# A Fourier mixing and ELU kernel on one core: where the first weight pieces are summed, where two buffers are cleared, and the order of scratch writes and x loads

## The chip, the cores and the metric

The kernel runs on one core of one Trainium2 chip. A core has a matrix engine (TensorE, PE in the profile; its weight loads are PEld), VectorE (DVE), ScalarE (ACT), GpSimd (POOL) and SyncE (SP), which here only issues transfers; 16 DMA engines move the data. The metric is the device time of one execution in microseconds (us).

## What is computed

The reference is a Fourier filter along the sequence followed by a two-layer block with an ELU between the layers:

```python
X = np.fft.rfft(x, axis=1)                     # x: 8 x 3008 x 256
y = np.fft.irfft(X * (filt_r + 1j * filt_i), n=3008, axis=1)
h = y.reshape(24064, 256) @ w_in               # 256 x 2048
g = np.where(h > 0, h, np.exp(np.minimum(h, 0)) - 1)
out = g @ w_out                                # 2048 x 256
```

w_in and w_out arrive as float64. The kernel turns them into float32 itself, from the two 32-bit halves of each number.

## The kernel before

**Batches and quads.** The 8 batches go through two halves: the filter, and the two-layer block. The second half is the long one and runs without pause; the filter of batch b + 1 is spread over it. The block is cut into items (b, m, q): 8 batches, 6 groups of tokens m, 4 quarters q of the 2048 hidden columns. The program calls the place of an item in that list a *quad*; 24 quads make a batch (`PER`), and a quad takes about 13 us. In quad i TensorE runs the seven up products of item i (`up_steps`: Strassen-like, L541) interleaved with the seven down products of item i - 1 (`down_steps`, L623). The letters U and D in L981 and L990 give the interleaving. Each quad's VectorE work contains four adds that rebuild blocks of h from products (L549: b11, b22, b21 and so on), four ELU maxima (L563), and four operations that prepare the next factors (L599 to L603); ScalarE copies products out of PSUM (L552) and computes the exponentials (L558, L559). The add of b22 (L549) reads the product accumulated in `phd`, and TensorE's last up product of the quad (s4) goes on accumulating into the same bank: TensorE waits for that add.

**A plan written by hand.** Everything else is put into quads with `at(quad, place, function, ...)`. Place 2 comes after the third of the U and D steps of the quad, place 3 after the fifth, place 0 in the middle, place 1 at the end. Within the program all engines follow program order, each its own instructions, so the plan decides what stands ahead of what on VectorE, ScalarE, POOL and SP.

**Weights.** They come in 16 pieces k = 4q + j. For j of 0 and 1 a piece belongs to `w_in[q]`, for 2 and 3 to `w_out[q]`. `w_fetch(k)` loads it; `w_split(k)` (L708, L709, VectorE) separates mantissa and exponent bits; `w_float(k, *parts)` (L718, ScalarE) has four steps numbered 0 to 3 that turn them into floats; `w_join(k, parts)` (L724 to L739, VectorE) puts sign and exponent together (part 0) and multiplies into the weight tile (part 1); `w_sums(k, engine, parts)` (L743 to L750) makes the four sums that the Strassen-like scheme needs, on 128 x 256 each, on the engine given. In the first 85 us (the *boot* part) batch 0 goes through the filter on its own while pieces 0 to 11 are made; pieces 12 to 15 are finished in quads 0 to 3. Piece 11's sums are used by the down products in quad 3, piece 13's by the up products in quad 3, piece 15's by the down products in quad 4.

**The filter of later batches.** For batch b, with t = 24 (b - 1): `x_load(b, c)` (L199 to L215) loads one of six slices c with seven transfers on SP (one table, six, or five, of x); `x_unit` (L217) makes a sum and a difference on VectorE; `a_unit` (L227) multiplies two slices on TensorE (psa) and ScalarE copies the result out (L238); `z_write` (L302) writes it to a scratch tensor z in DRAM with two transfers on SP. The slices lie in four buffers, so a load has to wait until `a_unit` has read the slice that is four earlier. When all six slices are written, `z_read` (L310) reads z transposed, eight transfers for two groups, and `b_unit` (L375) multiplies them on TensorE with 40 small matmuls (pf, L383) in quad t + 6. `f_read` (L321) reads the filter on POOL into the buffers `fbufs`, two of which have to be zero outside the rows that are read; `f_pairs` (L771) prepares that filter in DRAM with transfers on SP in quads 1 to 4. For batch 1 the units of slices 0 to 5 lie in quads 2, 2, 3, 3, 4, 4; for later batches in t + 0, 0, 3, 3, 4, 4.

The loop that the change reorders stands at L937 to L945: per slice it plans x_unit, a_unit for every second slice, then the load of the slice four ahead, then the scratch write.

**The end of the boot part.** `y_write_first(g)` (L365) writes the filter's result to the scratch yd; its last transfer is issued by ScalarE. `y_read(0, 0)` (L473) and `n_unit(0, 0)` (L483, matmuls psn, evictions y at L492) follow, then `n_sums` (L516 to L519, VectorE), and with quad 0 the two-layer block begins. Seven warm-up matmuls (L901) stand between.

Of the kernel before, what the change touches and what calls it, by code (L numbers as in the profile page):

```python
# [28 lines left out]
B = 8  # L29
# [4 lines left out]
NXC = H // XC  # L34
NG = K2 // 4
XBUFS = 4
# [95 lines left out]
def kernel(  # L132
# [9 lines left out]
    nc = tc.nc  # L142
# [34 lines left out]
    fbufs = [fall[:, i] for i in range(FBUFS)]  # L177
# [502 lines left out]
    def w_fetch(k, queue=nc.gpsimd):  # L680
        q, j = divmod(k, 4)

        if k in (3, 4, 14, 15):
            wd = t2[:, k % 11 - 3].rearrange("p u d -> p (u d)")
        elif k == 10:
            wd = t1p.tile([P, XC, D], FP32, tag="t1", name="wd").rearrange("p u d -> p (u d)")
        elif k in (6, 7, 8, 9):
            wd = xp.tile([P, 2, 2, D], FP32, tag="xc", name="wd").rearrange("p k u d -> p (k u d)")
        else:
            wd = fbufs[{5: 0, 11: 0, 12: 1, 13: 2}.get(k, k)].rearrange("p c u d -> p (c u d)")  # L690
        wd = wds[k] = wd.bitcast(U32).rearrange("p (a w) -> p a w", w=2)
        if j < 2:
            srcs = [moe_w_in.bitcast(U32)[ts(j, P), ts(q, 1024)]]
        else:
            srcs = [moe_w_out.bitcast(U32)[ts(4 * q + 2 * (j - 2) + i, P), :] for i in range(2)]
        for i, s in enumerate(srcs):
            n = 512 // len(srcs)
            queue.dma_start(wd[:, ts(i, n), :].rearrange("p a w -> p (a w)"), s)
# [6 lines left out]
    def w_split(k):  # L705
        m, e, f, l = wts[k] = wtmp[{9: 2, 10: 1, 11: 0, 12: 3, 13: 4, 15: 5}.get(k, k % 2)]
        hi = wds[k][:, :, 1]
        nc.vector.tensor_scalar(out=m, in0=hi, scalar1=0x000FFFFF, scalar2=None, op0=ALU.bitwise_and)  # L708
        nc.vector.tensor_scalar(out=e, in0=hi, scalar1=0x7FF00000, scalar2=None, op0=ALU.bitwise_and)  # L709

    def w_float(k, *parts):
        m, e, f, l = wts[k]
        ef = e.bitcast(FP32)
        steps = ((l, wds[k][:, :, 0], AXT.Identity, 2.0 ** -52, 0.0), (f, m, AXT.Identity, 2.0 ** -20, 1.0),
                 (ef, e, AXT.Relu, -8.0, edges[:, 0:1]), (e, ef, AXT.Relu, -1.0, edges[:, 1:2]))
        for i in parts or range(4):
            o, x, func, scale, bias = steps[i]
            nc.scalar.activation(out=o, in_=x, func=func, scale=scale, bias=bias)  # L718

    def w_join(k, parts=(0, 1)):  # L720
        q, j = divmod(k, 4)
        m, e, f, l = wts[k]
        if 0 in parts:
            nc.vector.scalar_tensor_tensor(out=e, in0=wds.pop(k)[:, :, 1], scalar=0x80000000, in1=e,  # L724
                                           op0=ALU.bitwise_and, op1=ALU.bitwise_or)
            nc.vector.tensor_tensor(out=f, in0=f, in1=l, op=ALU.add)
        if 1 not in parts:
            return
        e = e.bitcast(FP32)
        if j < 2:  # L730
            f, e = (t.rearrange("p (a j c) -> p a j c", a=2, j=2) for t in (f, e))
            dst = w_in[q][:, 2 * j:2 * j + 2, :, :].rearrange("p j a c -> p a j c")
            nc.vector.tensor_tensor(out=dst, in0=f, in1=e, op=ALU.mult)
        else:

            f, e = (t.rearrange("p (i a e s) -> p i e a s", i=2, a=4, e=2) for t in (f, e))
            dst = w_out[q][:, 0:4, j - 2, :].rearrange("p (i e) (a s) -> p i e a s", i=2, a=4)
            for i in range(2):
                nc.vector.tensor_tensor(out=dst[:, i], in0=f[:, i], in1=e[:, i], op=ALU.mult)  # L739
        if j % 2 == 1 and k < 7:  # L740
            w_sums(k)

    def w_sums(k, engine=nc.vector, parts=(0, 1, 2, 3)):  # L743
        q, j = divmod(k, 4)
        w = (w_in if j < 2 else w_out)[q]
        a11, a21, a12, a22, s1, s2, s4 = (w[:, i] for i in range(7))
        sums = ((s1, a21, a22, ALU.add), (s2, s1, a11, ALU.subtract), (s4, a12, s2, ALU.subtract), (a21, a11, a21, ALU.subtract))
        for i in parts:
            o, x, y, op = sums[i]
            engine.tensor_tensor(out=o, in0=x, in1=y, op=op)  # L750
# [30 lines left out]
    with tc.manual_schedule():  # L781


        with tc.tile_pool(name="boot", bufs=1) as bp:
# [68 lines left out]
            c = t1p.tile([P, XC, D], FP32, tag="t1", name="wfl").rearrange("p (a b) d -> p a (b d)", a=2)  # L853
            places(c[:, 0], flat(tnp.tile([P, 4, P], FP32, tag="tn", name="we")), c)
            for t in (zq, rq):
                t = t.rearrange("p a u d -> p a (u d)")
                places(t[:, 0], t[:, 1], t[:, 2:4])
            t = t3f.rearrange("p a (b u) d -> p (a b) (u d)", u=2)
# [1 line left out]
            w_split(7)  # L860
            w_join(6)
            w_split(8)
            floats = {0: (7, 0, 1), 1: (7, 2, 3), 2: (8, 0, 1), 3: (8, 2, 3), 4: (9, 0, 1), 5: (9, 2, 3), 6: (10, 0, 1), 7: (10, 2, 3)}
            for g in range(4):
                t_first(g)
            for g in range(NG + 2):
# [20 lines left out]
            y_read(0, 0, slice(0, K2 - 4), slice(K2 - 4, K2))  # L887
            for k in (14, 15):
                w_fetch(k, nc.sync)
            w_join(8)  # L890
            for k in (11, 12, 13):
                w_split(k)
# [2 lines left out]
            w_sums(9)  # L895
            w_join(10)
            w_join(11)
            w_sums(11, nc.gpsimd)
            warm = psO.tile([P, 512], FP32, tag="po2", name="warm")
            for k in range(7):  # L900
                nc.tensor.matmul(warm, w_in[0][:, 0, 0, :], w_in[0][:, 0:2].rearrange("p a b c -> p (a b c)"),  # L901
# [15 lines left out]
        def at(quad, place, fn, *a):  # L917
            plan.setdefault((quad, place), []).append((fn, a))


        for quad, place, fn, *a in ((0, 0, w_split, 14), (1, 2, w_join, 12), (1, 2, w_split, 15), (1, 2, w_float, 14, 0, 1),
                                    (1, 3, w_float, 14, 2, 3), (2, 2, w_float, 15, 0, 1), (2, 3, w_float, 15, 2, 3),
                                    (2, 0, w_join, 14, (0,)), (2, 1, w_join, 14, (1,)), (2, 1, w_join, 15),
                                    (3, 0, w_sums, 15, nc.vector, (0, 1, 2)), (3, 1, w_sums, 15, nc.vector, (3,))):
            at(quad, place, fn, *a)
        for c in range(2, XBUFS):
# [3 lines left out]
            for u in range(2):  # L930
                at(1 + 2 * c + u, 0, f_pairs, c, u)
        for i in range(2):
            at(2 + i, 1, nc.gpsimd.memset, fbufs[i], 0.0)
        for b in range(B):
            t = (b - 1) * PER
            if b > 0:
                for c, s in enumerate((2, 2, 3, 3, 4, 4) if b == 1 else (0, 0, 3, 3, 4, 4)):  # L937
                    at(t + s, 0, x_unit, b, c)
                    if c % 2 == 0:
                        opens.add(t + s + 1)  # L940
                        at(t + s, 1, a_unit, b, c)
                    nb, nxt = (b, c + XBUFS) if c + XBUFS < NXC else (b + 1, c + XBUFS - NXC)
                    if nb < B:
                        at(t + s, 1, x_load, nb, nxt)
                    at(t + s, 1, z_write, b, c)  # L945
                for g in range(0, NG, 2):
                    s = t + 6 + 2 * g
                    opens.update((s + 1, s + 4))
                    for k in (g, g + 1):
                        at(s - 2, 1, f_read, b, k)  # L950
                        at(s - 1, 0, z_read, b, k)
                    at(s, 1, b_unit, b, g)
                    at(s + 1, 2, re_mult, b, g)
                    at(s + 1, 1, re_sums, b, g)
                    parts = ((0, 0), (0, 1), (1, 0), (1, 1))
                    early = 3 if g == 6 else 4
                    at(s + 2, 2, im_mult, b, g, *parts[:early])
                    at(s + 2, 1, im_mult, b, g, *parts[early:])
                    at(s + 2, 1, im_join, b, g)
                    at(s + 3, 2, im_sums, b, g)  # L960
                    at(s + 3, 1, bi_unit, b, g)
                    at(s + 3, 1, y_write, b, g)
            for m, (s, place) in enumerate(((23, 0), (25, 1), (29, 1), (32, 0), (36, 0), (40, 0))):
                if b > 0 or m > 0:
                    at(t + s - 2, 0, tn_read, b, m)
                    at(t + s - 2, 1 if m == 0 else 0, y_read, b, m)
                    at(t + s, place, n_unit, b, m)

                    at(*((t + s + 1, 1) if m > 2 else (t + s, place)), n_sums, b, m)
                if b == 0 and m == 1:  # L970
                    at(1, 1, w_join, 13)
                    at(1, 1, w_sums, 13, nc.gpsimd)
                at(t + PER + 4 * m + 5, 0, c_unit, b, m)
                at(t + PER + 4 * m + 6, 0, o_unit, b, m)

        items = [(b, m, q) for b in range(B) for m in range(6) for q in range(4)]
        for i in range(-PER, len(items) + 3):
# [3 lines left out]
            for n, k in enumerate("DUUDUDDU" if i in opens else "UUDUDDU"):  # L981
                s = ups if k == "U" else downs
# [7 lines left out]
            for k in "DUUDUD" if i in opens else "DUUDUDD":  # L990
                s = ups if k == "U" else downs
# [40 lines left out]
```

## Time and profile before

| what | value |
|---|---|
| median of the runs | 2592.95 us (runs: 2590.71, 2592.95, and a disturbed one of 9503.64) |
| the profiled execution's own time | 2593.74 us |
| its span, first to last instruction | 2591.9 us |
| mean granted TensorE clock | 0.993 of full |
| TensorE busy | 2551.7 us, 98% |
| VectorE, ScalarE, POOL busy | 79%, 60%, 7% |
| DMA, mean | 80 GB/s |

How to read the profile lines below. A line of the timeline has the start in us from the span's start, the duration in us, the engine (SPq and ACTq are the queues that issue transfers), the source line, the operation, output<-input by the program's names, shape, and the number of instructions that were merged; in brackets stands how long the engine had been idle and what it waited for. Matmuls are pipelined and their ends are modelled. A line of the windows has the window, its length, then busy time and number of instructions of PE, PEld, DVE, ACT and POOL, the granted clock, the busy share of the DMA engines and the GB/s.

### The profile page before, as it was taken

How to read it: one execution, taken by the hardware profiler on the slowest of the kernel's cores; microseconds unless marked ns; L12 is line 12 of the kernel's file. 1: busy time of each engine (PE TensorE's matmuls, PEld its weight loads, DVE VectorE, ACT ScalarE, POOL GpSimd, SP SyncE). 2: the span in 40 equal slices, each digit the busy share in tenths (PEclk: the TensorE clock that was granted, in tenths of full speed). 3: DMA queues.
4: the chain of work that ended last, by engine and by line, in shares of the span. 5: the costliest groups of instructions: out<-in, count | busy, mean ns of one | idle time of the engine just before them, and what ended most of it. 6: DMA issues, size and time to landing. Idle time of an engine off the chain costs nothing.

```text
span 2591.9 us, 39471 instructions
## 1 busy us (share of the span) xinstructions
PE 2551.7 (98%) x14474; PEld 2204.0 (85%) x14474; DVE 2041.2 (79%) x3524; ACT 1548.1 (60%) x2713; POOL 169.1 (7%) x325
## 2 busy tenths in 40 slices
PE   6899999999999999999999999999999999999998
PEld 4688889888898888988889888888889888898887
DVE  6868887788877888788886888778887788866666
ACT  6755556656566655665556656566655655555554
POOL 5100100010000000000000000000000010000000
PEclk8999999999999999999999999999999999999999
DMA  9662213422234231433215231243213322110010
GB/s 282 169 184 69 70 36 88 129 70 63 51 100 108 61 78 42 119 81 76 62 44 151 63 84 37 78 122 84 61 43 87 91 60 68 37 49 20 21 29 17
DMA packets 229177, 206.35 MB, mean 80 GB/s; under 512 B 128666, under 2 KB 195418, under 8 KB 228984
## 3 DMA queue, kind: packets, MB, share of 16 engines
q1 hardware_dynamic: 213624, 172.94, 26.2%
q0 software_dynamic: 14000, 30.44, 4.3%
q8 instruction: 114, 1.87, 0.3%
q10 hardware_dynamic: 1360, 0.46, 0.1%
q14 instruction: 79, 0.65, 0.1%
HBM read 131.87 MB, written 78.17 MB: 81 GB/s over the span
## 4 chain that ended last, share of the span: by engine, by line
PE 96%; DMA 2%; DVE 1%; ACT 0%; issue 0%; SPq 0%; DVEq 0%; ACTq 0%
PE po L623 44%; PE phs L541 25%; PE phd L541 13%; PE pha L541 6%; PE psn L490 3%; PE psa L234 2%; PE pf L383 2%; PE pv L455 1%; DMA xc<-in_x_dram 1%; DMA x<-in_x_dram 0%; PE po L330 0%; DMA yd<-t 0%; PE po L296 0%; PE psr L330 0%; DMA t<-yd 0%
## 5 line engine op out<-in xcount | busy, mean ns | idle before, releaser
L623 PE MATMUL po<-g,wo 128*128 128x256 f32 (+1 forms) x5376 | 1315.1, 377 | 0.0
L623 PEld LDWEIGHTS po<-g,wo 128*128 128x128 f32 x5376 | 1013.6, 190 | 163.6 <-issue 49.7
L552 ACT ACTIVATE g<-phs 128x512 f32<-128x512 f32 (+1 forms) x576 | 339.0, 589 | 751.6 <-PE phs L541 750.2
L559 ACT ACTIVATE e<-e 128x512 f32<-128x512 f32 (+1 forms) x768 | 477.2, 621 | 24.4
L549 DVE TENSOR_TENSOR g<-phd,g 128x512 f32<-128x512 f32 (+1 forms) x384 | 259.6, 676 | 293.6 <-ACT e L559 205.1
L541 PE MATMUL phs<-ys,wi 128*128 128x256 f32 (+1 forms) x1536 | 387.6, 375 | 2.0 <-ACT g L552 1.5
L541 PE MATMUL phs<-y,wi 128*128 128x256 f32 (+1 forms) x1536 | 388.5, 375 | 0.0
L563 DVE SCALAR_TENSOR_TENSOR g<-e,g 128x512 f32<-128x512 f32 (+1 forms) x576 | 387.3, 672 | 0.3 <-ACT e L559 0.2
L558 ACT ACTIVATE e<-g 128x512 f32<-128x512 f32 (+1 forms) x576 | 353.4, 614 | 46.7 <-DVE g L549 38.1
L541 PEld LDWEIGHTS phs<-ys,wi 128*128 128x128 f32 x1536 | 291.4, 190 | 36.0 <-ACT g L552 3.0
L541 PEld LDWEIGHTS phs<-y,wi 128*128 128x128 f32 x1536 | 288.2, 190 | 35.8 <-ACT g L552 0.2
L563 DVE SCALAR_TENSOR_TENSOR g<-e,phs 128x512 f32<-128x512 f32 (+1 forms) x192 | 130.0, 677 | 140.3 <-ACT e L559 139.9
L541 PE MATMUL phd<-ys,wi 128*128 128x256 f32 (+1 forms) x768 | 196.2, 378 | 3.1 <-DVE g L549 3.1
L541 PE MATMUL pha<-y,wi 128*128 128x256 f32 (+1 forms) x768 | 194.0, 375 | 0.0
L541 PE MATMUL phd<-y,wi 128*128 128x256 f32 (+1 forms) x768 | 193.7, 375 | 0.0
L558 ACT ACTIVATE e<-phs 128x512 f32<-128x512 f32 (+1 forms) x192 | 113.0, 589 | 128.7 <-PE phs L541 128.7
L541 PEld LDWEIGHTS phd<-ys,wi 128*128 128x128 f32 x768 | 145.0, 191 | 24.1 <-DVE g L549 8.2
L541 PEld LDWEIGHTS pha<-y,wi 128*128 128x128 f32 x768 | 145.6, 190 | 17.5 <-ACT y L492 0.2
L541 PEld LDWEIGHTS phd<-y,wi 128*128 128x128 f32 x768 | 145.8, 190 | 16.5
L324 POOL DMA_DIRECT2D fall<-fp x224 | 110.5, 501 | 733.4 <-DVE r L428 704.3
L549 DVE TENSOR_TENSOR g<-pha,g 128x512 f32<-128x512 f32 (+1 forms) x192 | 129.3, 673 | 25.9 <-PE pha L541 25.7
L600 DVE TENSOR_TENSOR g<-g,g 128x512 f32<-128x512 f32 (+1 forms) x192 | 130.7, 681 | 6.6
(155 smaller groups left out, 2097.8 us busy)
## 6 DMA issues: line engine op xcount, KB each, us to landing
yd<-t SPq DMA_DIRECT2D x127, 192.0 KB
t<-yd SPq DMA_DIRECT2D x47, 512.0 KB
z<-t SPq DMA_DIRECT2D x84, 256.0 KB
fall<-fp POOLq DMA_DIRECT2D x224, 96.0 KB, 3.0
t<-z SPq DMA_DIRECT2D x224, 96.0 KB
out_dram<-o SPq DMA_DIRECT2D x632, 32.0 KB
tn<-tn_t SPq DMA_DIRECT2D x48, 256.0 KB
xc<-in_x_dram SPq DMA_DIRECT2D x84, 128.0 KB
```

The costliest lines, as they stand in the source:

```text
L234: nc.tensor.matmul(p[o:o + 64, u, :], w[r, u, o:o + 64], src[r, u, :], start=True, stop=True)
L324: nc.gpsimd.dma_start(t[32 * a:32 * a + 24].rearrange("p c u d -> p (c u d)"), fp[g, a].rearrange("q c u d -> q (c u d)"))
L383: nc.tensor.matmul(pf[p][1][32 * a:32 * a + 32, js, :], fb[r, v, :], t2[r, js, a, :], start=True, stop=True, tile_position=(32 * p, 32 * a))
L490: nc.tensor.matmul(ps[:, ts(q, P)], t[:, i - 4 * m, ds(dh * P, P)], w[:, i - 4 * m, :], start=True, stop=True)
L541: nc.tensor.matmul(ps[:, a, 0:h], w_in[q][:, COMBO[n], a, :], y[n], start=start and a == 0, stop=True, skip_group_check=True)
L549: nc.vector.tensor_tensor(out=g[o], in0=i0, in1=i1, op=ALU.add)
L552: nc.scalar.activation(out=g[o], in_=i0, func=AXT.Copy)
L558: nc.scalar.activation(out=e, in_=src, func=AXT.Relu, scale=-1.0)
L559: nc.scalar.activation(out=e, in_=e, func=AXT.Exp, scale=-1.0)
L563: nc.vector.scalar_tensor_tensor(out=g[n], in0=es[n], scalar=1.0, in1=src, op0=ALU.subtract, op1=ALU.max)
L600: nc.vector.tensor_tensor(out=b12, in0=b22, in1=b12, op=ALU.subtract)
L623: nc.tensor.matmul(po[i][:, u, 0:h], w_out[q][:, COMBO[n], a, :], g[n][:, a, :], start=q == 0 and a == 0 and n in (1, 3, 6, 4), stop=True, ...
```

## The change

Five edits, all in the boot part and in the plan:

- The sums of piece 11 move from POOL, at the end of the boot part, to VectorE in the middle of quad 0. The sums of piece 13 move from POOL, at the end of quad 1, to VectorE in quad 2, after the third step.
- The steps 2 and 3 of `w_float` for piece 10, on ScalarE, move from the loop over g (at g = 7) to after the last fetches of the boot part.
- `w_join(14)` is done in one go at the end of quad 2; before, its first part stood in the middle of quad 2.
- The two buffers of the filter are cleared by ScalarE in quad 3, after the third and the fifth step; before, by POOL at the end of quads 2 and 3.
- Per pair of slices, both scratch writes are planned first and both loads after them; before, load and write alternated.

On the engines this comes out so: VectorE has eight more operations of 128 x 256, POOL eight fewer and two memsets fewer, ScalarE two more of 128 x 1024, SP the same transfers in another order in every batch, TensorE the same matmuls in the same order. In quad 2, VectorE's order from the add of b11 to the add of b22 was: first part of the join of 14 (L724, L726), four operations of x_unit; it is now: four sums of piece 13 (L750), four operations of x_unit. At the end of quad 2 the whole join of 14 now stands ahead of the join of 15.

```diff
-            floats = {..., 6: (10, 0, 1), 7: (10, 2, 3)}
+            floats = {..., 6: (10, 0, 1)}
...
             for k in (14, 15):
                 w_fetch(k, nc.sync)
+            w_float(10, 2, 3)
             w_join(8)
...
             w_join(11)
-            w_sums(11, nc.gpsimd)
...
-        for quad, place, fn, *a in ((0, 0, w_split, 14), (1, 2, w_join, 12), ...
+        for quad, place, fn, *a in ((0, 0, w_split, 14), (0, 0, w_sums, 11), (1, 2, w_join, 12), ...
-                                    (2, 0, w_join, 14, (0,)), (2, 1, w_join, 14, (1,)), (2, 1, w_join, 15),
+                                    (2, 2, w_sums, 13), (2, 1, w_join, 14), (2, 1, w_join, 15),
...
         for i in range(2):
-            at(2 + i, 1, nc.gpsimd.memset, fbufs[i], 0.0)
+            at(3, 2 + i, nc.scalar.memzero, fbufs[i])
...
-                    nb, nxt = (b, c + XBUFS) if c + XBUFS < NXC else (b + 1, c + XBUFS - NXC)
-                    if nb < B:
-                        at(t + s, 1, x_load, nb, nxt)
-                    at(t + s, 1, z_write, b, c)
+                    if c % 2:
+                        for k in (c - 1, c):
+                            at(t + s, 1, z_write, b, k)
+                        for k in (c - 1, c):
+                            nb, nxt = (b, k + XBUFS) if k + XBUFS < NXC else (b + 1, k + XBUFS - NXC)
+                            if nb < B:
+                                at(t + s, 1, x_load, nb, nxt)
...
                     at(1, 1, w_join, 13)
-                    at(1, 1, w_sums, 13, nc.gpsimd)
```

## The prediction

> **What bounds the kernel now.** I read the page's busy shares first, then TensorE's waits, then the windows and the timeline of the only places where it loses time.
>
> ```profile
> PE 2551.7 (98%) x14474; PEld 2204.0 (85%) x14474; DVE 2041.2 (79%) x3524; ACT 1548.1 (60%) x2713; POOL 169.1 (7%) x325
> ```
>
> TensorE is busy for 98% of the span, and TensorE's waits from 140 us to the end are an empty list. Batches 2 to 7 offer nothing; 2% (52 us, about what a measurement of this kernel can tell from no change) is more than all 40 us of idle TensorE. What can move lies ahead of 190 us, at three places. The first two show in windows whose edges I set where the granted clock changes (columns: window, its length, busy us of PE, PEld, DVE, ACT, POOL, granted clock, DMA share, GB/s):
>
> ```profile
> 80.85:84.27 3.42, 2.10 (x5) 0.57 (x3) 3.32 (x9) 3.39 (x7) 0.00 (x0) 1.00 0.77 185
> ...
> 114.99:118.40 3.41, 1.31 (x7) 0.96 (x6) 3.34 (x5) 1.12 (x2) 3.41 (x4) 1.00 0.00 0
> 118.40:121.81 3.41, 2.45 (x7) 2.23 (x8) 2.52 (x6) 1.15 (x2) 0.28 (x1) 0.53 0.00 0
> 121.81:125.23 3.42, 3.42 (x19) 2.37 (x21) 3.35 (x7) 1.15 (x2) 0.00 (x0) 0.50 0.00 0
> 179.85:183.26 3.41, 3.40 (x37) 0.84 (x35) 2.11 (x4) 0.00 (x0) 0.00 (x0) 1.00 0.46 99
> 183.26:186.67 3.41, 3.41 (x9) 2.74 (x10) 2.12 (x4) 2.13 (x6) 0.00 (x0) 0.53 0.17 31
> ```
>
> Twice, after a stretch in which TensorE had little to do, the clock is halved, for 6.8 and 3.4 us. The timeline says why TensorE starved in quad 2:
>
> ```profile
> 112.77 4.13 POOL L750 TENSOR_TENSOR wi<-wi 128x256 f32<-128x256 f32 x4 [22.55 <-DVE wi L733]
> ...
> 113.97 1.21 DVE L726 TENSOR_TENSOR wfl<-wfl 128x512 f32<-128x512 f32 x1
> ...
> 115.10 1.21 DVE L220 TENSOR_TENSOR sd<-xc 128x512 f32<-128x512 f32 x1
> ...
> 116.84 1.84 POOL L999 MEMSET fall<- 128x1024 f32 x2
> 117.37 0.68 DVE L220 TENSOR_TENSOR sd<-xc 128x512 f32<-128x512 f32 x1
> 118.08 0.69 DVE L221 TENSOR_TENSOR xc<-xc 128x512 f32<-128x512 f32 x1
> 118.69 0.62 DVE L549 TENSOR_TENSOR g<-phd,g 128x448 f32<-128x448 f32 x1
> ...
> 119.36 0.74 PE L541 MATMUL phd<-ys,wi 128*128 128x224 f32 x1 [3.06 <-DVE g L549]
> ```
>
> While POOL does the sums of piece 13, VectorE's operations take 1.00 to 1.21 us instead of 0.68; beside POOL's memset they do not. The add that TensorE needs (L549) is behind them: 3.06 us lost. And in quad 6:
>
> ```profile
> 170.81 1.72 SPq L308 DMA_DIRECT2D z<-t  x2
> 175.76 3.17 SPq L314 DMA_DIRECT2D t<-z  x8
> ...
> 178.91 4.34 PE L383 MATMUL pf<-t,pairs 24*32 24x256 f32 x40
> ...
> 181.68 0.13 PEld L383 LDWEIGHTS pf<-t,pairs 24*32 24x32 f32 x2 [0.49 <-DMA t<-z]
> ```
>
> The 40 small matmuls wait for reads of the scratch z, which SP issued only once the last scratch write had landed. The same group takes 1.72 us in batch 2 (496.01) and later.
>
> **The change, part by part.** Against the profiled execution (2593.74 us, span 2591.9).
>
> *Quad 0: sums of piece 11, and the late floats.* POOL's four sums (3.22 us from 86.42) go; beside them L518 and L519 took 0.91 and 0.80 us, against 0.42 each in quad 1, and TensorE waited 0.42 for L518, then for ScalarE's evictions behind it. At most 0.9 comes back. VectorE gains 4 x 0.42 = 1.7 us after w_split(14), where it idled 1.63 us before the next L549, and it arrives 0.9 earlier: hidden; uncovered it would delay that add by up to 1.7. Against this, w_float(10, 2, 3) (two operations, 1.48 us) moves behind the last yd write on ScalarE. Before the move it delays evictions that wait for TensorE anyway (L362 at 76.50), so the write itself is perhaps 0.1 earlier; after it, floats 11 to 13 all run 1.3 later, and the eviction of y (86.31, with 0.74 idle before it) may start up to 0.5 later. w_join(10) reads it at 82.26, long after. Bounds -0.6 to +0.9, taken +0.4: the contention is measured, the idle absorbs most of the rest.
>
> *Quad 2: sums of piece 13, join of 14.* Before, from the add of b11 at 112.51 to that of b22 at 118.69: 6.18 us. After: the add 0.54 (start to start), four sums 1.67 (three take 1.25 at 129.83), four x_unit operations 2.66 (0.72, 0.61, 0.72, 0.61, by the rows from 131.08), no contention: 4.87. TensorE's gap falls by 1.31, from 3.06 to 1.75, and it restarts at R = 118.05 in place of 119.36. The half clock cost half of 119.36 to 125.23, 2.95 us. In the windows above it came after 1.31 busy out of 3.41; elsewhere 1.56 and 1.58 busy were also followed by half clock (26.24 and 16.00 us), 2.10 was not. A gap of 1.75 leaves at least 1.66: if it lies wholly in one window the clock may fall once more, otherwise not. I take not, and price the other below.
>
> The whole join of 14 now stands ahead of the join of 15, so what is late next is quad 3. From R: the add of b21 at +0.96, L563 at +1.75 (ScalarE's two operations ahead of it), L599 to L603 until +5.2, two joins of 2.0 each to +9.2, the add of b11 and three sums to +11.0, x_unit to +13.65, add of b22, and TensorE 0.67 after its start: R+14.3. TensorE's own work to that point is 135.83 - 119.36 - 2.95 = 13.5. A new stall of 0.8 to 0.9. Net of quads 2 and 3: 135.83 - (118.05 + 14.3) = 3.5 gained. Bounds: 1.0 (a halved clock in both places) to 6.0 (no stall at all).
>
> *Clearings.* Two ScalarE operations of 128x1024: 128x4096 took 3.62 us (L807), so about 0.9 each. They fall into ScalarE's idle 1.73 and 1.72 us ahead of L552 at 130.73 and 133.00: nothing, and up to 1.8 on TensorE if that cover were gone. POOL loses 1.84 us of memset that slowed nobody. f_read on POOL, which needs the cleared buffers, waits for fp anyway (POOL idles 17.6 us ahead of 163.77).
>
> *Scratch writes ahead of x loads.* On SP, per pair, the two writes of the even c pass its seven x-load issues, those of the odd c pass fourteen. In quad 2 SP now waits first for ScalarE's copies (L238, done 2.9 to 3.9 us after psa starts at 124.14) where it waited for TensorE (1.8); behind it stand x loads, f_pairs and the reads of tn and y. x loads of (1,4) and (1,5), issued 1.8 to 11.4 us after psa starts, will be issued 5.0 to 13.1 after; x_unit wants them 18.65 after (142.79): covered. In quads 4 and 5 the last write is issued some 8 us earlier; the z reads wait no longer for its landing (from 172.53 to 175.76) but for SP alone, which comes to them about 4.5 us earlier. DMA is full from 157 to 174.5 (0.8 to 1.0 in 1-us windows) with the same bytes; then the reads need about 6 us, as now, of which some three overlap. They land some 53.5 us after psa starts; TensorE gets to pf 54.8 to 55 after. So the group falls to its 1.72: 2.62 gained, and half of 3.41 us of half clock, 1.7, together 4.3. Bounds: 0 (reads as late as now) to 4.4. In later batches the same move meets no wait of TensorE: nothing; loads issued in quad 0 are used in quad 4.
>
> Sum: 0.4 + 3.5 + 4.3 = 8.2; 2593.74 - 8.2 = **2585.5 us**. The runs shown are 2590.71 to 2592.95 (the third, 9503.64, aside), so the profiled one stands 0.8 above the median; the median less 8.2 would be 2584.8, within the range.
>
> The Trainium skill ("TensorE: Matmul & The Clock Gate", section "HAM oscillation") gives the rule that TensorE is throttled by idle gaps of more than about 3.4 us. The trace disagrees: a gap of 3.06 us, and a group that was merely slowly fed, were each followed by half clock. By the rule the 4.65 us of half clock had other causes and would stay: 2590.2, an estimate from that page; by the rows 2585.5.
>
> **Rivals.**
> 1. *The z reads stay late.* DMA was full until 174.5 whatever the order, and eight reads then have to queue behind x loads. For it: shares of 0.9 and more; against it: it idled at 175 (0.02). Then 4.3 is lost: 2589.8.
> 2. *The clock halves again.* A 1.75 us gap in quad 2, or the pause before the first real matmuls (82.95 to 85.10, where the warm-up matmuls may end a little sooner), falls in one window: 1.7 us each, less the 0.9 stall of quad 3 that the first absorbs: 2586.3 to 2588.
> 3. *VectorE is the bound throughout quads 0 to 3, and the reads stay late too*: only 1 to 2 us: 2592.
> 4. *Slower: the later x loads starve quad 4.* If (1,4) or (1,5) lands more than 18.65 us after psa starts, x_unit waits; VectorE has 2.27 us idle and 0.7 of lead there, so TensorE stalls past 21.6. To cancel 8.2 they must land about 29 after (26 with 3 us of half clock); at 33 it is 2597. Issued by 13.1, with DMA at 0.6 to 0.95, that needs a tenfold delay.
>
> **How the numbers follow.** Forecast as summed, rival 2 within it: 0.72, own range 2582.5 to 2588; rival 1: 0.16; rival 3: 0.07; rival 4: 0.05. Range 2582 to 2591: the low end is the sum with the upper bounds of quads 2 and 3 and quad 0 (11.3 off), the high end takes in rival 1 with the clock falling once. No case reaches 52 us: faster 0.01, same 0.98, slower 0.01.
>
> **What would show it.** Right: in quad 2 the add of b22 starts 4.9 us after that of b11, TensorE waiting under 2 us there and up to 1 us in quad 3, no half clock around 118 to 125; t<-z issued ahead of 171, pf in batch 1 at 1.7 us, clock 1.00 after it; L518 at 0.42. Wrong: pf still over 3 us; x_unit of quad 4 waiting for a DMA; a halved clock at a new place; any wait of TensorE past 200 us.

## The result, and the profile after

The changed kernel takes a median of **2586.67 us** (8 runs, 2584.12 to 2588.76), the kernel before beside it 2592.95 us (7 runs, 2590.71 to 2597.54, with a disturbed one of 9503.64 left out). The ratio is **0.9975, with a 95% interval from 0.9964 to 0.9987**: some 6.5 us, far within 2%. The forecast was 2585.5. The profiled execution took 2586.76 us (before 2593.74), its span is 2585.0 (2591.9), its mean granted clock 0.996 (0.993).

The page's busy times, in the order of the line shown of before (engine, busy us, share of the span, instructions):

```profile
PE 2543.5 (98%) x14474; PEld 2199.1 (85%) x14474; DVE 2040.2 (79%) x3532; ACT 1550.4 (60%) x2715; POOL 159.7 (6%) x315
```

VectorE has its eight sums more, some 3.4 us, and is busy 1.0 us less in all: the operations that were slowed beside POOL's sums in the two places are short again, which gives some 2.8 back, and the rest is small differences over all its other operations. The timeline of quads 2 and 3 after the change:

```profile
113.45 0.62 DVE L549 TENSOR_TENSOR g<-pha,g 128x448 f32<-128x448 f32 x1
113.98 1.67 DVE L750 TENSOR_TENSOR wi<-wi 128x256 f32<-128x256 f32 x4
115.57 0.68 DVE L220 TENSOR_TENSOR sd<-xc 128x512 f32<-128x512 f32 x1
...
117.61 0.69 DVE L221 TENSOR_TENSOR xc<-xc 128x512 f32<-128x512 f32 x1
118.22 0.61 DVE L549 TENSOR_TENSOR g<-phd,g 128x448 f32<-128x448 f32 x1
...
118.89 1.02 PE L541 MATMUL phd<-ys,wi 128*128 128x224 f32 x4 [1.66 <-DVE g L549]
...
132.53 0.61 DVE L549 TENSOR_TENSOR g<-phd,g 128x448 f32<-128x448 f32 x1
...
133.20 1.02 PE L541 MATMUL phd<-ys,wi 128*128 128x224 f32 x4 [0.60 <-DVE g L549]
```

From the add of b11 (113.45) to that of b22 (118.22) it is 4.77 us, where it was 6.18; the gap of TensorE is 1.66 where it was 3.06, and quad 3 has a stall of 0.60 that was not there. The window that holds the new gap, and the one after it, have full clock (the eighth column is the granted clock):

```profile
115.97:119.38 3.41, 1.75 (x10) 1.40 (x9) 3.34 (x7) 1.12 (x2) 0.00 (x0) 1.00 0.00 0
119.38:122.79 3.41, 3.41 (x39) 2.76 (x41) 3.28 (x6) 2.57 (x5) 0.00 (x0) 1.00 0.00 0
```

And in quad 6 (SP's issues of the last scratch writes and of the reads, then the 40 small matmuls):

```profile
155.09 3.60 SPq L308 DMA_DIRECT2D z<-t  x4
...
169.21 4.18 SPq L314 DMA_DIRECT2D t<-z  x8
...
176.38 1.72 PE L383 MATMUL pf<-t,pairs 24*32 24x256 f32 x40
```

The reads go out 7.2 us ahead of the matmuls (3.15 before), and the group takes its 1.72 in place of 4.34.

Where the time went can be laid out over five points that both timelines have: the start of the warm-up matmuls (A), the last up product of quads 0, 2 and 3 (B, C, D: the line of `phd` that waits for the add of b22), and the pf group of batches 1 and 2 (E, F). A is a time from the span's start; A-B and the others are differences of starts, all in us; e1 to e9 are experiments below. Each line is one profiled execution, and some of these lie at an edge of their kernel's runs: e1's took 2587.11 us (median 2591.01), e5's 2584.50 (2587.26).

| profile | A | A-B | B-C | C-D | D-E | E-F | span |
|---|---|---|---|---|---|---|---|
| before | 76.67 | 16.73 | 25.96 | 16.47 | 43.08 | 317.10 | 2591.9 |
| after | 77.43 | 16.90 | 24.56 | 14.31 | 43.18 | 312.79 | 2585.0 |
| e1, reorder alone | 76.30 | 17.65 | 25.97 | 13.54 | 43.08 | 312.81 | 2585.3 |
| e9, all but the reorder | 77.55 | 16.44 | 24.56 | 14.31 | 43.18 | 314.26 | 2586.2 |
| e5, floats put back | 76.19 | 15.75 | 24.56 | 14.31 | 43.18 | 312.81 | 2582.7 |
| e7, joins 12 and 13 earlier | 74.85 | 17.14 | 22.73 | 14.29 | 43.18 | 312.81 | 2580.9 |

From before to after: 0.76 lost ahead of A, 0.17 in A-B, 3.56 gained in B-C and C-D, 0.10 lost, 4.31 gained in E-F; together 6.84, and the spans differ by 6.9. After F nothing differs.

### The profile page after: what moved, and what is told of

Its sections match the earlier page's. It is cut to its first block, busy times and chain, and to the rows that moved or that the text cites. A ratio compares the mean times of both kernels' runs of the same rounds, so it can differ in the third digit from the quotient of the medians.

```text
span 2585.0 us, 39447 instructions
## 1 busy us (share of the span) xinstructions
PE 2543.5 (98%) x14474; PEld 2199.1 (85%) x14474; DVE 2040.2 (79%) x3532; ACT 1550.4 (60%) x2715; POOL 159.7 (6%) x315
## 4 chain that ended last, share of the span: by engine, by line
PE 96%; DMA 2%; DVE 1%; ACT 0%; issue 0%; SPq 0%; DVEq 0%; ACTq 0%
PE po L623 44%; PE phs L541 25%; PE phd L541 13%; PE pha L541 6%; PE psn L490 3%; PE psa L234 2%; PE pf L383 1%; PE pv L455 1%; DMA t<-in_moe_w_in_dram 1%; DMA wd<-in_moe_w_out_dram 1%; DMA xc<-in_x_dram 0%; DMA yd<-t 0%; PE po L330 0%; PE po L296 0%; PE psr L330 0%
```

## The experiments

The theory: three places gave the time, the add of b22 in quad 2, the half clock behind it, and the reads of z with their half clock. The rivals: that one edit carries it all, and that the half clock belonged to the profiled run and not to the kernel. Ratios are to the kernel before, beside it on the same chip, with 95% intervals.

**e1: the reorder on SP alone.** The kernel before, with only the loop of L937 to L945 changed as in the diff (both writes first, then both loads).

> The kernel before with nothing but the new order of scratch writes and x loads. My theory: quads 0 to 3 are as before (TensorE waits about 3.1 us for the add of b22 in quad 2, half clock after it), but the z reads are issued 4 to 6 us earlier relative to the psa matmuls, the pf group of batch 1 takes 1.72 us instead of 4.34, and no half clock follows it: about 4.3 us less than the kernel before, ratio 0.9983. Rival (the reads are late because DMA is full, or only because VectorE's edits moved the rest): pf stays at 4 us and the half clock after it stays: ratio 1.000.

Measured: median 2591.01 beside 2593.41, ratio 0.9984 [0.9973, 0.9995]. In quads 2 and 6 its timeline reads:

```profile
119.92 1.02 PE L541 MATMUL phd<-ys,wi 128*128 128x224 f32 x4 [3.08 <-DVE g L549]
...
170.01 3.68 SPq L314 DMA_DIRECT2D t<-z  x8
...
176.54 1.72 PE L383 MATMUL pf<-t,pairs 24*32 24x256 f32 x40
```

The reorder by itself brings pf to 1.72. In quad 2 there is the same gap of 3.08 us as before, and no half clock after it (C-D is 13.54 against 16.47). Two windows of 3.41 us share the gap:

```profile
115.10:118.51 3.41, 1.75 (x10) 1.40 (x8) 3.38 (x4) 1.50 (x3) 3.33 (x5) 1.00 0.00 0
118.51:121.92 3.41, 2.00 (x10) 2.00 (x11) 3.28 (x7) 1.43 (x3) 0.72 (x1) 1.00 0.00 0
```

In the profiled run of before the half clock begins at 118.62, so the window ahead of it held 2.3 of the 3.06 us:

```profile
115.21:118.62 3.41, 1.09 (x6) 0.74 (x4) 3.34 (x4) 1.12 (x2) 3.41 (x4) 1.00 0.00 0
118.62:122.03 3.41, 2.67 (x7) 2.45 (x8) 2.52 (x6) 1.26 (x3) 0.06 (x1) 0.50 0.00 0
```

So the same gap costs 2.9 us more or not, depending on where the windows fall.

**e9: everything but the reorder.**

```diff
 # the changed kernel, load and scratch write alternating as before
-                    if c % 2:
-                        for k in (c - 1, c):
-                            at(t + s, 1, z_write, b, k)
...
+                    if nb < B:
+                        at(t + s, 1, x_load, nb, nxt)
+                    at(t + s, 1, z_write, b, c)
```

> The changed kernel with loads and scratch writes alternating again, as before. My theory: the z reads wait for the last scratch write's landing again; TensorE reaches pf 43.2 us after the stalled product of quad 3, and the reads land about 58 us after psa of quad 2 starts, so the group takes about 4.3 us and half clock may follow: 2.6 to 4.4 us slower than the changed kernel. Rival (the loads finish in time once quads 2 and 3 are cured): pf at 1.72 us and the same time.

Measured: 2586.84 beside 2593.78, ratio 0.9974 [0.9964, 0.9984]: not to be told from the whole change.

```profile
164.66 2.84 SPq L308 DMA_DIRECT2D z<-t  x2
...
171.84 3.17 SPq L314 DMA_DIRECT2D t<-z  x8
...
176.04 2.85 PE L383 MATMUL pf<-t,pairs 24*32 24x256 f32 x40
```

With quads 2 and 3 cured, the last writes are issued at 164.66 in place of 170.81 even in the old order, the reads 4.2 us ahead of pf, and pf takes 2.85. No half clock follows. The reorder is worth 1.1 in pf and 1.47 in E-F (314.26 against 312.79), in profiles; the medians do not show it. By these two profiles, one of each kernel, the late reads of before were in part a consequence of what happened in quads 2 and 3. In the other profiles, which all have the reorder, pf takes 1.72 to 1.79. As to the rival that one edit carries it all: the reorder alone gives 0.9984 and the other four edits together 0.9974, while the whole gives 0.9975, so the two do not add up.

**e2, e3, e4: the two edits of quad 2, as a square.** e2 puts the sums of 13 back on POOL, e3 splits the join of 14 again, e4 does both; the rest is the changed kernel.

```diff
 # e2
-                                    (2, 2, w_sums, 13), (2, 1, w_join, 14), ...
+                                    (2, 1, w_join, 14), ...
                     at(1, 1, w_join, 13)
+                    at(1, 1, w_sums, 13, nc.gpsimd)
 # e3
-                                    (2, 1, w_join, 14), (2, 1, w_join, 15),
+                                    (2, 0, w_join, 14, (0,)), (2, 1, w_join, 14, (1,)), (2, 1, w_join, 15),
```

> The changed kernel, but the sums of piece 13 are back on POOL at the end of quad 1; the join of 14 stays whole at the end of quad 2. My theory: between the adds of b11 and b22 in quad 2 VectorE has 1.67 us less of its own to do and loses 1.3 to 1.7 us to POOL, so the interval stays at 4.6 to 4.9 us, TensorE's gap at 1.4 to 1.7 us, no half clock, and the time is that of the changed kernel within 0.5 us. Rival (the move off POOL is what cured quad 2): the interval is above 6 us, the gap about 3 us, half clock follows: 3 us slower than the changed kernel.

> The changed kernel, but the first part of the join of 14 (two operations, 1.3 us) is back in the middle of quad 2; the sums of piece 13 stay on VectorE. My theory: the interval between the adds of b11 and b22 grows by 1.3 to about 6.1 us, TensorE's gap to about 3.0 us, the stall in quad 3 goes (0.6 us), and if the gap falls mostly into one window the clock halves for 3.4 or 6.8 us: 0.7 us slower than the changed kernel without half clock, 2.5 to 3.5 us with it. Rival (the sums' place is what counts): gap about 1.7 us as in the changed kernel and the same time.

> The changed kernel with both of quad 2 as before: sums of piece 13 on POOL, the first part of the join of 14 in the middle of quad 2. Both theories: interval between the adds about 6.2 us, gap about 3 us, as in the kernel before (the clearings stay on ScalarE and should not matter). It closes the square of the two edits: by my theory the join alone makes the difference of 1.3 us in the gap, by the rival the sums alone. pf of batch 1 stays at 1.72 us.

Measured: e2 2585.96, ratio 0.9973 [0.9962, 0.9984]; e3 2587.91, 0.9979 [0.997, 0.9989]; e4 2588.22, 0.9984 [0.9974, 0.9993]. TensorE's gap in quad 2, from the profiles:

| | join of 14 in one go | join of 14 split |
|---|---|---|
| sums of 13 on VectorE | 1.66 (after) | 2.87 (e3) |
| sums of 13 on POOL | 1.74 (e2) | 3.07 (e4) |

The join decides the gap. (The ratios do not tell these kernels from the changed one: all four intervals overlap.) e2's timeline has the contention in full and loses nothing by it:

```profile
111.23 0.62 DVE L549 TENSOR_TENSOR g<-pha,g 128x448 f32<-128x448 f32 x1
111.77 1.00 DVE L220 TENSOR_TENSOR sd<-xc 128x512 f32<-128x512 f32 x1
112.80 1.10 DVE L221 TENSOR_TENSOR xc<-xc 128x512 f32<-128x512 f32 x1
113.82 1.21 DVE L220 TENSOR_TENSOR sd<-xc 128x512 f32<-128x512 f32 x1
115.07 1.10 DVE L221 TENSOR_TENSOR xc<-xc 128x512 f32<-128x512 f32 x1
116.09 0.61 DVE L549 TENSOR_TENSOR g<-phd,g 128x448 f32<-128x448 f32 x1
```

Four x_unit operations take 4.32 us start to start beside POOL's sums (111.77 to 116.09); without, they take 2.65 (115.57 to 118.22 in the changed kernel), behind 1.59 of sums. What POOL's sums steal from VectorE equals the time that VectorE needs to do them itself. The Trainium skill ("SBUF — State Buffer", section "Who interferes with whom") says that a VectorE operation that reads two SBUF operands contends with GpSimd operations that read SBUF and not with those that only write: the rows agree, 1.00 to 1.21 beside the sums and 0.68 beside the memset. The same section calls the shared ports an exclusive lock; in these rows neither engine stands still for a whole operation of the other, and both are slowed: POOL's sums take 1.05 to 1.17 us each beside these operations, and 0.72 to 0.73 in e11 where VectorE had nothing to do.

The split join also brings e3 a clock penalty: the window that holds its gap of 2.87 has TensorE busy for 0.68 us, and half clock follows. e4 has half clock behind its gap too, for 3.41 us from 124.73.

```profile
117.39:120.80 3.41, 0.68 (x4) 0.33 (x2) 3.34 (x6) 1.09 (x2) 0.00 (x0) 1.00 0.00 0
120.80:124.21 3.41, 3.27 (x9) 2.95 (x10) 2.52 (x6) 1.83 (x4) 0.00 (x0) 0.50 0.00 0
```

**e6: the clearings back on POOL.**

```diff
-            at(3, 2 + i, nc.scalar.memzero, fbufs[i])
+            at(2 + i, 1, nc.gpsimd.memset, fbufs[i], 0.0)
```

> The changed kernel with both clearings back on POOL at the end of quads 2 and 3. My theory: nothing moves: the memsets slow no VectorE operation (0.68 us beside them in the kernel before), the interval between the two adds of quad 2 stays at 4.8 us, the gap at 1.7 us, time the same within 0.3 us. Rival (the memsets take part in the contention): the interval grows by 0.5 us or more.

Measured: 2586.94, ratio 0.9978 [0.9968, 0.9987], B-C 24.58, C-D 14.31. The clearings are worth nothing that shows. In the changed kernel they lie on ScalarE ahead of evictions that wait for TensorE all the same:

```profile
125.51 1.05 ACT L989 ACTIVATE fall<-fall 128x1024 uint32<-128x1024 uint32 x1
127.34 0.54 ACT L552 ACTIVATE g<-phs 128x448 f32<-128x448 f32 x1 [0.78 <-PE phs L541]
```

After 1.05 us of clearing ScalarE still idles for 0.78 before TensorE has the product ready.

**e5: the floats of piece 10 back in the loop over g.**

```diff
-            floats = {..., 6: (10, 0, 1)}
+            floats = {..., 6: (10, 0, 1), 7: (10, 2, 3)}
...
-            w_float(10, 2, 3)
```

> The changed kernel, but steps 2 and 3 of the floats of piece 10 are back in the loop at g = 7. My theory: from the start of the warm-up matmuls to the yd write on ScalarE it takes 0.2 to 0.3 us longer (about 0.95 to 1.0 instead of 0.74), and ScalarE has an idle pause again before the first eviction of y, so that this eviction starts when psn is done and not up to 0.5 us later; the two cancel: the time is that of the changed kernel within 0.5 us. Rival (this edit is why the change gave 1.2 us less than forecast): quad 0 is reached 0.5 to 1 us sooner relative to the warm-up matmuls and the time falls by that.

Measured: 2587.26, ratio 0.9977 [0.9967, 0.9987]; A-B 15.75 in the profile. The floats meet TensorE's path at the eviction of y. First e9, which has the changed kernel's boot part, then e5:

```profile
85.56 2.02 PE L490 MATMUL psn<-tn,t 128*128 128x128 f32 x16 [1.73 <-DMA t<-yd]
...
86.17 1.46 ACT L718 ACTIVATE rq<-rq,edges 128x512 f32<-128x512 uint32 x2
...
87.53 0.95 ACT L492 ACTIVATE y<-psn 128x448 f32<-128x448 f32 x2
```

```profile
84.25 2.02 PE L490 MATMUL psn<-tn,t 128*128 128x128 f32 x16 [1.78 <-DMA t<-yd]
...
85.46 0.54 ACT L492 ACTIVATE y<-psn 128x448 f32<-128x448 f32 x1 [0.55 <-PE psn L490]
```

In e9 the eviction starts directly behind a float, with no idle time, 1.97 us after psn; in e5 ScalarE idles 0.55 us waiting for TensorE, and the eviction comes 1.21 after psn. This delay is 1.77 to 2.35 in e2, e4, e6 and e9, so there the moved floats hold the eviction back by 0.6 to 1.1. In the profile of the changed kernel itself they hardly do (1.32): psn, which waits for a DMA, started 9.12 us after A, against 7.61 to 8.16 in those five. By A-B the move of the floats costs some 0.8 us (16.56, the mean of e2, e4, e6, e9 and the changed kernel, against 15.75; e3 and e8 had half clock there). That rests on one profile of e5, in a stretch that scatters as much: before and e1 have the same boot part, and their A-B are 16.73 and 17.65. The medians do not show it: A itself lies between 74.85 and 81.00 in the profiles of this study, though no edit moves anything on TensorE ahead of it.

**e11: sums of 11 back on POOL as well** (e5 and `w_sums(11, nc.gpsimd)` behind `w_join(11)`; one run).

> The changed kernel with the floats of piece 10 back in the loop and the sums of piece 11 back on POOL at the end of the boot part. From the start of the warm-up matmuls to the last up product of quad 0 the kernel before took 16.7 us, the changed kernel with only the floats back 15.75. My theory (the sums on POOL slow L516 to L519 to 0.5 to 0.9 us each, and TensorE waits for them): 16.7 here. Rival (the sums' place is worth nothing there): about 15.8.

Measured: 2590.4, A-B 18.46, and undecided: the start of the block had half clock in this run (from 88.32 to 91.73), and the operations that POOL's sums should have slowed came later than the sums. These ran from 89.07 to 92.30; L517 to L519 began at 92.74 and took 0.38 to 0.39, and L516, beside the last sum, took 0.39 too.

```profile
88.61 3.51 PE L490 MATMUL psn<-tn,t 128*128 128x128 f32 x16 [3.02 <-issue]
```

The 16 matmuls take 2.02 at full clock. What the move of these sums is worth by itself was not settled; before and e1, which differ from e5 in the boot part and quad 0 by it, stand at 16.73 and 17.65, e5 at 15.75. What the profiles do show is the wait: TensorE waited 0.42 (before) and 0.85 (e1) for L518, which took 0.91 beside the sums, and had no such wait with the sums on VectorE.

**e8: the x loads later, to price the slower rival.** The loads of (1,4) and (1,5) are planned a quad later.

```diff
-                                at(t + s, 1, x_load, nb, nxt)
+                                at(t + s + (b == 1 and c == 1), 1, x_load, nb, nxt)
```

> The changed kernel with the loads of slices (1,4) and (1,5) planned one quad later still, which puts them behind quad 3's reads of the filter, tn and y on SP. By the pricing of the slower rival: they are issued about 20 us after psa of quad 2 starts instead of 5.6 to 12.9 and land at about 29 to 30; past 21.6 every us is a us of TensorE's, so TensorE stalls 7 to 9 us in quad 4 and the clock halves after it: 9 to 12 us slower than the changed kernel, near 2597. If loads are hidden in some other way (x_unit does not sit ahead of the add of b22, or they land sooner), less than 3 us.

Measured: 2588.13, ratio 0.9981 [0.9972, 0.999]. The loads went out 13.7 to 20.7 us after psa starts (123.23), not 20 and more, since SP, without them ahead, came to the f_pairs transfers and the reads behind those earlier. They landed at 143.79 and 147.44, as the waits of x_unit show:

```profile
143.79 0.69 DVE L220 TENSOR_TENSOR sd<-xc 128x512 f32<-128x512 f32 x1 [1.57 <-DMA xc<-in_x_dram]
...
147.44 0.69 DVE L220 TENSOR_TENSOR sd<-xc 128x512 f32<-128x512 f32 x1 [2.23 <-DMA xc<-in_x_dram]
...
149.51 1.13 PE L541 MATMUL phd<-ys,wi 128*128 128x256 f32 x4 [0.85 <-DVE g L549]
```

20.6 and 24.2 us after psa, then, and TensorE lost 0.85. The mechanism exists; the expected 9 to 12 us did not come. In the changed kernel these loads went out 5.6 to 12.9 after psa (127.00 to 134.27, psa at 121.36), and x_unit waited for none.

**e7: joins of 12 and 13 earlier.** The gap of quad 2 starts with VectorE's delay in quad 1, so the join of 12 goes into the boot part and that of 13 into its place.

```diff
             w_join(11)
+            w_join(12)
...
-(1, 2, w_join, 12)
+(1, 2, w_join, 13)
...
-                    at(1, 1, w_join, 13)
```

> The changed kernel, but the join of piece 12 is done at the end of the boot part and the join of 13 takes its place in quad 1, so that VectorE has 2.0 us less at the end of quad 1, from where it never idles until quad 3. My theory (VectorE is the bound from the end of quad 1 to quad 3, and only there): the gap of 1.7 us in quad 2 and the stall of 0.6 us in quad 3 go, L516 in the boot part starts 0.6 us later because the join fills VectorE's idle 1.4 us there and overshoots it: 1.5 us faster than the changed kernel. Rival (TensorE's product n = 7 or ScalarE sets the add of b22): the gap stays above 1 us and the time does not fall, or rises by 0.6 us.

Measured: median **2583.88** (2581.82 to 2585.58) beside 2592.45, ratio 0.9963 [0.995, 0.9977], the fastest kernel of the study. The wait in quad 2 is gone, and one in quad 3 is all that is left of TensorE's waits for the adds:

```profile
PE phd L541 <- DVE g L549: 0.7, 1, 0.7
```

```profile
114.72 0.93 PE L541 MATMUL phd<-ys,wi 128*128 128x224 f32 x4
...
129.01 1.02 PE L541 MATMUL phd<-ys,wi 128*128 128x224 f32 x4 [0.68 <-DVE g L549]
```

B-C falls by 1.83. The stall of quad 3 was expected to go too and did not: C-D is 14.29 here, 14.31 in the changed kernel. C-D is 14.29 to 14.31 in all nine profiles that have the whole join of 14 at the end of quad 2: from C on, VectorE's own work up to the next add of b22 sets it, however early C comes. Against the changed kernel the gain shows in the segments; the two ratios' intervals overlap.

**e10: e7 with the floats put back.**

> The kernel with the joins of 12 and 13 moved up, and steps 2 and 3 of the floats of piece 10 back in the loop. With the joins moved up, VectorE reaches L516 last in the boot part, 0.65 us after the eviction of y; so by my theory the floats' place no longer matters: from the warm-up matmuls to the last up product of quad 0 about 17.1 us as without it, the same time within 0.3 us. Rival (the floats cost ScalarE time that counts in any case): 0.8 us less there.

Measured: 2586.13, ratio 0.9969 [0.9958, 0.9981]; B-C 22.73, as in e7. In its profile the first matmuls of the block ran at half clock and A-B was 17.54, so it does not say what the floats are worth there.

```profile
86.92 2.94 PE L490 MATMUL psn<-tn,t 128*128 128x128 f32 x16 [1.97 <-DMA t<-yd]
```

**The clock over all runs.** Each run lists its span and mean granted clock. The 69 runs of the kernel before that were made beside the experiments spread from 0.991 to 0.998. By clock (runs, median span):

| clock | before | after |
|---|---|---|
| 0.991 | 1, 2602.2 | none |
| 0.992 | 3, 2596.0 | none |
| 0.993 | 6, 2594.6 | none |
| 0.994 | 17, 2592.0 | none |
| 0.995 | 16, 2591.4 | 1, 2583.7 |
| 0.996 | 18, 2589.8 | 5, 2585.0 |
| 0.997 | 7, 2588.9 | 2, 2585.2 |
| 0.998 | 1, 2586.8 | none |

The profiled run of before, at 0.993, had lost more clock than 59 of the 69 (those at 0.994 or more). At equal clock, 0.996, the change is worth 4.8 us; the means over all runs are 0.9949 before and 0.9961 after. That difference, 0.0012 of 2590 us, is some 3 us, an estimate: up to half of the gain is clock that the runs of before lost more often.

## Why the prediction was right, step by step

- *Quad 2*, add to add 4.87 forecast, 4.77 measured; gap 1.75, and 1.66. Right in its sum, but the sum did not part the two edits, and the reading ahead of it named the slowed operations as the cause. The square shows that the four sums on VectorE cost what the contention cost. The 1.3 us come from the first part of the join of 14 being gone from that stretch.
- *Quad 3*, a new stall of 0.8 to 0.9 forecast, 0.60 measured, from the cause named: both joins ahead of the add of b11.
- *Net of quads 2 and 3*: 3.5 forecast, 3.56 measured, against the profiled run. 2.95 of it is the half clock of that run. e1 has the same gap without it, so it is a cost of some runs of the kernel before, not of each; against e1 the two quads gain 0.64 (B to D 39.51 there, 38.87 in the changed kernel), since the later start of the add in quad 3 takes back 0.77 of the 1.41 that the shorter gap gives.
- *Half clock after a gap of 1.75*: taken as not, and right. From 80 us on it followed windows with TensorE busy 0.68 to 1.45 (e10) out of 3.41 and none with 1.63 (e1, 80.95 to 84.36), 1.69 (e2) or more, the group pf of before aside. A gap of 1.66 leaves at least 1.75, so by these rows quad 2 alone no longer brings it about, wherever the windows fall. The prediction's windows lie 0.2 us ahead of the clock's own, which is why its first row of half clock has 0.53: in the right one TensorE was busy 1.09, not 1.31.
- *Reads of z*: pf 1.72 forecast and measured; issued ahead of 171 forecast, at 169.21 measured. But the 4.3 were given to the reorder alone. e9 shows that the cure of quad 2 without the reorder takes pf from 4.34 to 2.85 and ends the half clock in its profile; the reorder adds about 1.5. The two terms were not independent, and their sum is right only for both edits together.
- *Quad 0*: +0.4 forecast, -0.17 between the two profiles, and not settled. L518 and L519 take 0.39 as foreseen, and TensorE's wait for L518 is gone. The term let the floats delay the eviction of y by at most 0.5; that was too little, for they hold it back by 0.6 to 1.1 in e2, e4, e6 and e9. But A-B differs by 0.92 between before and e1, whose boot parts are the same, and against the mean of those two, 17.19, the mean of the changed boot part (16.56) is 0.6 lower. None of it shows in the medians.
- *Clearings*: nothing forecast; e6 shows nothing.
- *Ahead of A*: 0.76 lost, and in no term of the sum; A scatters by 6 us over the profiles, so this is the spread between runs and no effect of the change that these runs can show.
- *The total*: 8.2 was summed against the profiled run, and the segments give 6.8. Of the 8.2, 4.65 were half clock of that one run, and 59 of 69 runs of before lost less clock than it; that the forecast still lies 1.2 us from the median is in part luck.
- *The rivals*: reads that stay late did not occur in any profile with the reorder. A clock halving at the start of the block, which rival 2 priced at 1.7, occurs in two of the seven profiles that have the changed kernel's boot part (e3 and e8, with A-B 1.3 to 1.5 above the others), and in e10 and e11. The slower rival's deadline, 21.6 after psa, was a little too early: e8's second slice landed at 24.2 and cost 0.85, so TensorE's stall begins at about 23.3.
- *The skill's rule on the clock*: the Trainium skill ("TensorE: Matmul & The Clock Gate", section "HAM oscillation — how this bites in real kernels") throttles after idle gaps of more than about 3.4 us. Gaps of 2.87 (e3), 3.06 (before) and 3.07 us (e4) were followed by half clock here, and in the profile of the changed kernel none is left between 44.3 and 2580 us; by the rule the 4.65 would have stayed. The measurement decides for the rows.

What stays open: how much of the reorder's worth is left in the medians once quad 2 is cured (e9 and the changed kernel agree within their intervals), what the sums of piece 11 and the floats are worth by themselves, and how often the runs of before met the half clock, since only one of them has a profile.

## What to carry to other kernels

When a wait of the bottleneck engine lies behind several operations of another engine, first count what stands between its last two releases, and move out what nobody needs there; trading a slowdown against the same work done oneself gave nothing here. A penalty that depends on where a gap falls among fixed windows belongs to the run as much as to the kernel: compare the clocks of all runs before it is put into a sum. And where two losses lie one behind the other on the same queue, price the second with the first already cured.

## What was not expected of the hardware

- The clock is halved for whole windows of 3.41 us that lie on a fixed grid. In the profile of before it changes at 19.63, 26.46, 29.87, 43.52, 118.62, 125.44, 183.47 and 186.88 us, and all distances between these are whole multiples of 3.413.
- It does not go by the length of the idle gap alone: a 3.08 us gap that two windows share (1.75 and 2.00 busy) was free in e1, and a 3.06 us gap with 2.3 of it in one window (1.09 busy) cost before two windows at half clock. From 80 us on, 0.68 to 1.45 busy were followed by half clock and 1.63 or more were not, but for the window with the slowly fed pf group of before (busy 3.40, with modelled ends). Ahead of 80 us the busy time alone does not sort them: full clock followed 1.61 (e3, from 14.99), half clock 2.35 (e4, from 49.64). So these profiles show a line for idle gaps in the block, between 1.45 and 1.63, and no general threshold.
- The boot part scatters: the first warm-up matmul starts between 74.85 and 81.00 us, in profiles whose programs agree on TensorE up to there. It is larger than most of the steps tested.
